# A new written order for the first two chunks of an attention and gated feed-forward kernel

## The chip, the cores and the metric

The kernel runs on one core of one Trainium2 chip. The metric is the device time of one execution in microseconds. The engines are PE (TensorE), DVE (VectorE), ACT (ScalarE), POOL (GpSimd) and SP (SyncE), which issues most transfers; 16 DMA engines carry them. Each engine takes its instructions strictly in the order in which they were emitted.

## The reference

Two parts follow each other. The first is attention over 4 batches of 8 heads, 768 positions of 64 numbers: each position looks at its neighbours closer than 16 and at 24 block summaries (the largest key and the mean value of each block of 32). The second is a feed-forward layer whose hidden row is gated by a three-tap convolution.

```python
k_sum = k.reshape(B, H, nb, block, D).max(axis=3)
v_sum = v.reshape(B, H, nb, block, D).mean(axis=3)
scores_l = where(|i - j| < 16, scale * q @ k.T, -1e9)
scores_s = scale * q @ k_sum.T + log(block)
a = softmax(concat(scores_l, scores_s))
x = a @ concat(v, v_sum)                  # heads joined: (4, 768, 512)
h = maximum(x @ w_in, 0)                  # (4, 768, 1024)
conv = sum over k of conv_w[k] * h shifted by k - 1
out = (h * sigmoid(conv)) @ w_out         # (4, 768, 512)
```

## The kernel before, in words

The work is cut into 8 chunks: batch `c // 2`, first or second half of its positions. Attention goes by pairs of heads, four pairs to a chunk, so pair `n` belongs to chunk `n // 4`; 32 pairs in all. The contraction with `w_in` goes by eighths `u` of the hidden row, and each step `f c.u.cc` is three matmuls of 384 or 386 columns, one for each of the four quarters `cc` of the 512 inputs. The second contraction, with `w_out`, is three matmuls of 512 columns for each 128 positions and each eighth. Weights arrive as 64-bit floats and are taken apart on the chip into two 32-bit parts.

Chunks 0 and 1, together with the attention of pairs 8 to 13 and part of the second contraction of batch 0, are written out as one long string, `ORDER`, in which each word is one step. A function `run` (L542) turns a word into a call, and as the call stands under `manual_schedule` (L553) each engine gets its instructions in just this order. The words:

- `R`, `Q`, `T`, `K`, `V`, `M`, `O` are transfers issued by SP: the transposed keys of a pair (392 KB), its queries (192), its transposed values (384), its key windows (360), its value windows (288), the block means (72), and an eighth of `w_out` (512). `ks` (L268) takes the block maxima of the keys, `vs` (L283) the block sums of the values, both on DVE; `win`, `kb`, `vb` copy into the windows, `pv` and `vm` turn and scale the sums.
- `qk` is the 24 score matmuls of a pair; `mx` (L328, DVE) and `ex` (L343, ACT) are the softmax of a third of a head; `sm` and `rc` invert its sum, `nr` multiplies by it on POOL (`p`) or DVE (`v`); `tr` transposes a head's result on PE and `cp` copies it back on ACT (`a`) or DVE (`v`); `av` multiplies by the values; `xh`, `xl` take the result apart for the contraction.
- `f` as above; `re` rectifies, `ta` multiplies the middle tap (ACT or DVE), two `cv` (L458, DVE) add the outer ones, `th`, `mu`, `gh`, `gl` gate the row and take it apart. `g st.fc` is one step of the second contraction, `ob` stores.
- `zi`, `loi`, `sti`, `hii`, `wli` (and the same with `o`) take one eighth of the weights apart on ACT (L143), DVE (L154, L160), ACT (L175) and POOL (L180). `wN` is N matmuls on zeros, whose result is not used.

Ahead of `ORDER` stand 25 loads in a string of their own, `LOADS` (L559 to L563): keys, queries, values and value windows of pairs 0 to 3, all eight parts of `w_in` and the convolution's weights, and 10 matmuls on zeros.

Chunks 2 to 7 come from loops. `unit(c, u)` (L645) emits one eighth of a chunk. Through `slot(j)` (L571) it emits attention work for later pairs: an even slot the keys and values of pair `n + 2` (`R`, `K`, `T`) and the scores and softmax of pair `n`, an odd one the next queries, and for the first half of a batch `vs`, `pv`, `v_mean` and `k_max` of the pair to come. Here only PE keeps the written order. For SP, DVE, ACT and POOL a planner places the instructions by its own times, and it may put them between the steps of `ORDER` on the same engine, as their buffers allow. Buffers that matter: `kT` and `stage` have two each (`stage` is shared by the `T` loads from pair 8 on, the `O` loads and the key windows of pair 3), `kw` three, `va` and `q` four. A transfer that waits for its buffer holds up all behind it on SP.

Of the kernel before, what the change touches and what calls it, by code (L numbers as in the profile page):

```python
# [52 lines left out]
ex2.1.1 mx2.1.2 cp3a sti1 w1 qk3 O1 ex2.1.2 vs3 R8 hii1 av1 Q7 sm2 wli1 mx3.0.0 O5 rc2 pv3
ex3.0.0 mx3.0.1 R9 mx3.0.2 vm3 xh1 V5 loi2 w1 f0.1.0 ex3.0.2 xl1 nr2.0p M5 ex3.0.1 mx3.1.0
f0.1.1 zi2 vb3 mx3.1.1 mx3.1.2 tr4 zi3 f0.0.1 sti2 ex3.1.2 ex3.1.0 cp4v nr2.1p hii2 loi3 w3 tr5
ex3.1.1 wli2 zi5 sm3 cp5a sti3 w4 av2 zi6 rc3 hii3 loi6 f0.2.0 nr3.0v V6 xh2 wli3 tr6 M6 f0.2.1
cp6a nr3.1v zi7 xl2 kb4 w2 tr7 qk4 sti6 cp7a hii6 loi7 f0.0.2 K7 mx4.0.0 kb5 f0.2.2 ex4.0.0 Q8
sti7 av3 mx4.0.1 wli6 hii7 f0.1.2 ex4.0.1 V7 xh3 loi4 M7 zi4 mx4.0.2 kb6 xl3 wli7 ex4.0.2
# [12 lines left out]
gl0.4 ex7.1.2 f0.7.3 re0.6 mu0.5 tr13 O2 sm7 ta0.6a pv8 loo0 qk8 rc7 vm8 T10 sto0 cp13a f1.0.0
M8 re0.7 nr7.1p cv0.6.0 Q12 hio0 av6 mx8.0.0 K11 cv0.6.2 nr7.0p ta0.7a f1.0.1 mx8.0.1 ex8.0.0
V10 cv0.7.0 wlo0 xh6 tr14 mx8.0.2 zo2 cv0.7.2 ex8.0.2 cp14v g0.0 ex8.0.1 xl6 th0.7 tr15 loo2
g0.1 th0.6 mx8.1.0 O3 sto2 gh0.5 f1.0.2 ex8.1.0 cp15v gl0.5 hio2 mu0.6 av7 mx8.1.1 wlo2 gh0.6
mu0.7 f1.1.0 ex8.1.1 mx8.1.2 V11 vs10 xh7 qk9 gl0.6 ex8.1.2 gh0.7 xl7 f1.2.0 T9 zo3 loo3 K12
f1.0.3 mx9.0.0 gl0.7 sm8 Q13 pv10 ex9.0.0 f1.2.1 O6 re1.0 g0.2 sto3 vm10 ta1.0a M10 rc8 kb11
f1.2.2 mx9.0.1 hio3 nr8.1p cv1.0.0 f1.1.1 ex9.0.1 mx9.0.2 cv1.0.2 nr8.0p f1.2.3 ex9.0.2 mx9.1.0
f1.1.2 th1.0 vs9 wlo3 ex9.1.0 tr16 re1.2 f1.1.3 mx9.1.1 O7 mu1.0 cp16a pv9 kb12 g0.3 ta1.2a
mx9.1.2 re1.1 loo6 f1.3.0 gh1.0 cv1.2.0 tr17 ex9.1.1 gl1.0 ta1.1v g0.4 vm9 zo6 cp17v M9 qk10
cv1.1.0 ex9.1.2 T11 sm9 g0.5 sto6 zo7 Q14 cv1.1.2 f1.3.1 K13 hio6 rc9 av8 th1.1 loo7 mx10.0.0  # L80
wlo6 mu1.1 ex10.0.0 f1.3.2 mx10.0.1 xh8 V12 cv1.2.2 f1.4.0 ex10.0.1 M12 nr9.1p vs11 th1.2 g0.6
gh1.1 nr9.0p f1.4.1 mu1.2 xl8 gl1.1 f1.3.3 gh1.2 mx10.0.2 f1.5.0 ex10.0.2 sto7 tr18 re1.3 f1.5.1
mx10.1.0 gl1.2 ta1.3a cp18v f1.4.2 ex10.1.0 cv1.3.0 pv11 hio7 kb13 f1.5.2 mx10.1.1 cv1.3.2 vm11
wlo7 tr19 ex10.1.1 M11 f1.5.3 mx10.1.2 th1.3 cp19v qk11 ex10.1.2 mu1.3 re1.5 av9 sm10 gh1.3 rc10
K14 mx11.0.0 nr10.0p ta1.5a mx11.0.1 g0.7 mx11.0.2 ex11.0.1 M13 cv1.5.0 nr10.1p xh9 f1.6.0 V13
mx11.1.0 ex11.0.2 cv1.5.2 gl1.3 tr20 ex11.1.0 xl9 f1.6.1 ob0 cp20v f1.4.3 th1.5 mx11.1.1 tr21
ex11.0.0 mx11.1.2 g1.0 ex11.1.2 cp21v re1.4 f1.6.2 ex11.1.1 av10 ta1.4a sm11 cv1.4.0 f1.6.3 xh10
rc11 cv1.4.2 g1.1 nr11.0p re1.6 xl10 th1.4 qk12 nr11.1p ta1.6v mu1.4 g1.2 K15 cv1.6.0 gh1.4 tr22
# [658 lines left out]
```

## Time and profile before

| what | value |
|---|---|
| three runs | 397.14 us median, 397.09 to 398.24 |
| profiled execution | 396.87 us, span 395.1 us |
| PE busy | 376.2 us, 95% of the span |
| DVE, ACT, POOL busy | 252.4, 252.1 and 149.9 us |
| mean granted TensorE clock | 0.991 |
| bytes moved | 56.35 MB |

The span runs from the first to the last instruction; the profiled execution's own time is 1.8 us longer. A busy share is an average over stages with different limits: the written part takes about the first 118 us, the loops the rest. PE's busy time counts the matmuls on zeros too.

### The profile page before, as it was taken

Reading aid. Unit: us, or ns where it says so; the run is one execution under the profiler, and the core shown is the slowest. Engines: PE = TensorE matmul, PEld = TensorE weight load, DVE = VectorE, ACT = ScalarE, POOL = GpSimd, SP = SyncE. Lnnn points to the kernel's source line nnn. Section 1 sums busy time; section 2 is a strip of 40 time slices with the busy share of each in tenths; the row PEclk is TensorE's granted clock in tenths of the full one; section 3 lists DMA queues with packets and bytes.
Section 4 is the critical chain, followed back from the end, with each engine's and each line's share of the span. In section 5 each row is a group of like instructions: output and inputs, shape, how many; then the busy total and the mean of one; then the engine's idle time right before and its main releaser. Section 6 shows DMA issues by size and latency. Waiting matters only on the chain.

```text
span 395.1 us, 8807 instructions
## 1 busy us (share of the span) xinstructions
PE 376.2 (95%) x3148; PEld 315.2 (80%) x3154; DVE 252.4 (64%) x769; ACT 252.1 (64%) x792; POOL 149.9 (38%) x184
## 2 busy tenths in 40 slices
...
GB/s 279 347 379 335 255 309 207 268 241 246 265 209 146 117 95 139 190 144 164 111 107 74 127 69 97 118 105 123 104 37 28 29 0 28 27 28 27 27 55 53
DMA packets 27435, 56.35 MB, mean 143 GB/s; under 512 B 3136, under 2 KB 11520, under 8 KB 27392
## 3 DMA queue, kind: packets, MB, share of 16 engines
...
q8 instruction: 25, 0.41, 0.4%
...
HBM read 47.43 MB, written 6.29 MB: 136 GB/s over the span
## 4 chain that ended last, share of the span: by engine, by line
PE 70%; DVE 10%; DMA 8%; ACT 7%; POOL 2%; issue 2%; SPq 0%; ACTq 0%; POOLq 0%
PE f L508 30%; PE f L424 25%; PE xp L382 5%; PE pt L368 4%; PE pq L314 4%; DMA wo<-w_out 4%; DVE t L458 3%; ACT a L343 2%; DMA vt<-vT 2%; DMA kw<-k_win 1%; DVE ks L268 1%; POOL a L360 1%; PE pw L125 1%; DVE a L328 1%; ACT t L469 1%
## 5 line engine op out<-in xcount | busy, mean ns | idle before, releaser
L489 POOL TENSOR_TENSOR glo<-t,ghi 128x383 fp32r<-128x383 f32 (+1 forms) x64 | 65.8, 1029 | 122.4 <-ACT ghi L486 115.0
L424 PE MATMUL f<-xh,win_hi 128*128 128x384 f32 (+1 forms) x256 | 93.1, 364 | 2.8 <-DVE t L476 2.7
L458 DVE SCALAR_TENSOR_TENSOR t<-f,cw,t 128x382 f32<-128x382 f32 (+3 forms) x128 | 78.7, 615 | 14.5 <-ACT t L447 11.9
L424 PE MATMUL f<-xh,win_lo 128*128 128x384 f32 (+1 forms) x256 | 87.1, 340 | 0.3 <-POOL win_lo L180 0.3
L424 PE MATMUL f<-xl,win_hi 128*128 128x384 f32 (+1 forms) x256 | 87.1, 340 | 0.1
L343 ACT ACTIVATE a<-a,nm 128x120 f32<-128x120 f32 x192 | 73.8, 386 | 14.5 <-DVE nm L328 13.6
L508 PE MATMUL f<-wout_hi,ghi 128*128 128x512 f32 x192 | 76.3, 398 | 0.3 <-ACT ob L518 0.3
L508 PE MATMUL f<-wout_lo,ghi 128*128 128x512 f32 x192 | 75.3, 392 | 0.3 <-POOL wout_lo L180 0.3
L508 PE MATMUL f<-wout_hi,glo 128*128 128x512 f32 x192 | 74.9, 391 | 0.0
L469 ACT ACTIVATE t<-t 128x383 f32<-128x383 f32 (+1 forms) x64 | 33.4, 524 | 45.5 <-DVE t L458 44.4
L360 POOL TENSOR_TENSOR a<-a,sm 128x360 f32<-128x360 f32 x61 | 49.1, 826 | 31.5 <-ACT f L438 16.5
L424 PEld LDWEIGHTS f<-xh,win_hi 128*128 128x128 f32 x256 | 48.7, 190 | 8.2 <-DVE t L476 3.9
L476 DVE SCALAR_TENSOR_TENSOR t<-t,f 128x383 f32<-128x383 f32 (+1 forms) x64 | 35.4, 553 | 28.0 <-ACT t L469 27.7
L424 PEld LDWEIGHTS f<-xl,win_hi 128*128 128x128 f32 x256 | 48.8, 191 | 1.8 <-DVE xl L412 0.5
L424 PEld LDWEIGHTS f<-xh,win_lo 128*128 128x128 f32 x256 | 48.5, 190 | 0.8 <-POOL win_lo L180 0.8
L328 DVE CUSTOM_DVE_ANT_0 a<-pq,mask 128x120 f32<-128x120 f32 x192 | 44.6, 274 | 2.2 <-PE pq L314 2.2
L508 PEld LDWEIGHTS f<-wout_hi,glo 128*128 128x128 f32 x192 | 36.0, 188 | 7.9
L508 PEld LDWEIGHTS f<-wout_hi,ghi 128*128 128x128 f32 x192 | 36.1, 188 | 6.8 <-ACT ob L518 0.9
L508 PEld LDWEIGHTS f<-wout_lo,ghi 128*128 128x128 f32 x192 | 36.2, 188 | 5.7 <-POOL wout_lo L180 0.6
L486 ACT CAST ghi<-t 128x383 fp32r<-128x383 f32 (+1 forms) x64 | 32.5, 509 | 12.1 <-DVE t L476 11.8
L368 PE MATMUL pt<-ident,a 128*120 128x128 f32 x192 | 32.8, 279 | 6.7 <-ACT aT L373 2.8
L438 ACT ACTIVATE f<-f 128x384 f32<-128x384 f32 (+1 forms) x64 | 30.2, 473 | 14.0 <-PE f L424 13.5
...
## 6 DMA issues: line engine op xcount, KB each, us to landing
...
kT<-kT SPq DMA_DIRECT2D x12, 392.0 KB
vt<-vT SPq DMA_DIRECT2D x12, 384.0 KB
...
```

The costliest lines, as they stand in the source:

```text
L328: nc.vector.tensor_tensor_reduce(aa[n, h][:, i, :], pq[n][h][:, i * NK : (i + 1) * NK], mask[:, {(0, 0): 0, (1, 2): 2}.get((hf, i), 1), :] ...
L343: nc.scalar.activation(a, a, AF.Exp, bias=nm[n][:, h, i : i + 1], scale=-1.0, accum_out=sm[n][:, h, i : i + 1],)
L360: engine[e].tensor_tensor(a, a, sm[n][:, h, :].unsqueeze(2).to_broadcast([P, 3, NK]), ALU.mult)
L368: nc.tensor.transpose(pt[j][:NK, i * P : (i + 1) * P], a[:, i, :], ident)
L424: nc.tensor.matmul(f1ps[c, u][:, :n], w[:, u, cc, :], x[:, cc, :n], start=(cc == 0 and m == 0), stop=(cc == NCC - 1 and m == 2),)
L438: nc.scalar.activation(h, h, AF.Relu)
L458: nc.vector.scalar_tensor_tensor(t[:, i0:i1], f1ps[c, u][:, hf + k - 1 + i0 : hf + k - 1 + i1], cw[:, u, k : k + 1], t[:, i0:i1], ALU.mult ...
L469: nc.scalar.activation(t, t, AF.Tanh, scale=0.5)
L476: nc.vector.scalar_tensor_tensor(t, t, 1.0, h, ALU.add, ALU.mult)
L486: nc.scalar.copy(gate_rows("hi", c, u), conv[c, u])
L489: nc.gpsimd.tensor_tensor(gate_rows("lo", c, u), conv.pop((c, u)), gate_rows("hi", c, u).bitcast(F32), ALU.subtract,)
L508: nc.tensor.matmul(f2ps[b, st], g[:, fc, ss], w[:, fc, :], start=(fc == 0 and m == 0), stop=(fc == NFC - 1 and m == 2),)
```

## The change

The loads of `LOADS` move into `ORDER` as words of their own (`C` for the convolution's weights, `I` for the parts of `w_in`), and `ORDER` is written anew: the same steps in another order. The matmuls on zeros go from 10 + 56 to 12 + 35. Of 25 `cp`, 13 ran on DVE and 12 on ACT; now 10 and 15. Of 16 `ta`, 5 ran on DVE; now 4. All other steps are the same in number and on the same engines, though not always for the same pair.

The step functions that issue transfers, and `mu`, now return their instruction, and `run` keeps for each engine the last one returned: on SP the last load of `ORDER` (K15), on DVE mu1.7. In chunk 2 (`FIRST`), what `slot(j)` emits on these two engines is ordered behind them; `issue_after(x)` gives each instruction of the block that runs on the engine of `x` an edge to `x`, without a semaphore.

```diff
-LOADS = "k0 q0 k1 q1 v0 k2 q2 a0 v1 k3 q3 a1 w0 v2 c a2 w1 v3 a3 w2 w3 w4 w5 w6 w7"
-WARM = 10
+WARM = 12
...
 ORDER = """
-ks0 win0 kb0 qk0 ks1 win1 Q4 mx0.0.0 kb1 K4 ex0.0.0 mx0.0.1 mx0.0.2 ex0.0.1 vs0 ex0.0.2 win2
-mx0.1.0 w9 pv0 ks2 ex0.1.0 vm0 mx0.1.1 kb2 ex0.1.1 mx0.1.2 w5 qk1 vb0 ex0.1.2 sm0 rc0 vs1 nr0.1p
...
-ex12.1.1 xh11 qk13 ex12.1.2 xl11 ex12.1.0 f1.7.2 sm12 mx13.0.0 rc12 g1.6 ex13.0.0 mx13.0.1
-nr12.0p mx13.0.2 ex13.0.1 mx13.1.0 f1.7.3 ex13.0.2 nr12.1p mx13.1.1 mx13.1.2 ex13.1.0 g1.7
-ex13.1.2 tr24 ex13.1.1 ob1 cp24v sm13 re1.7 rc13 nr13.0p ta1.7a nr13.1p cv1.7.0 cv1.7.2 th1.7
-mu1.7 gh1.7 gl1.7
+R0 Q0 R1 I0 I1 R2 Q1 ks0 R3 win0 Q2 kb0 qk0 T0 ks1 win1 C kb1 zi0 loi0 T1 mx0.0.0 ex0.0.0
+mx0.0.1 mx0.0.2 sti0 zi1 I6 mx0.1.0 hii0 mx0.1.1 loi1 ex0.0.1 V0 win2 mx0.1.2 ex0.1.0 ks2 w12
+qk1 Q3 ex0.1.2 ex0.1.1 sti1 ex0.0.2 I2 mx1.0.0 kb2 sm0 hii1 mx1.0.1 win3 I4 mx1.0.2 rc0 ex1.0.0
+mx1.1.0 nr0.0p mx1.1.1 ex1.1.0 mx1.1.2 V1 ex1.0.2 vs0 nr0.1p w8 qk2 K4 ex1.0.1 ex1.1.1 wli1 ks3
+tr0 ex1.1.2 pv0 Q4 cp0a mx2.0.0 w1 tr1 mx2.0.1 ex2.0.0 kb3 mx2.0.2 wli0 vm0 vs1 T2 zcw zi6 cp1a
+mx2.1.0 w3 pv1 sm1 vb0 K5 mx2.1.1 ex2.0.1 locw mx2.1.2 ex2.1.0 rc1 w1 qk3 Q5 nr1.0v vm1 ex2.1.2
...
+rc2 sti2 xh0 ex3.0.0 nr2.0v O0 cp3a mx3.0.2 vb1 mx3.1.0 hii6 w4 tr4 mx3.1.1 V3 ex3.0.1 loi4 kb4
+mx3.1.2 cp4a T9 sti4 w2 qk4 hii2 xl0 nr2.1p ex3.1.0 I7 ex3.0.2 vs2 av1 wli6 ex3.1.2 ex3.1.1 I3
...
+gl1.5 xl10 f1.7.3 sm12 cp23a mx13.1.1 th1.6 g1.7 rc12 mx13.1.2 nr12.1p ex13.1.0 mu1.6 av11
+ex13.0.2 nr12.0p re1.7 gh1.6 ta1.7v tr24 ex13.1.2 gl1.6 cv1.7.0 ex13.1.1 ob1 cv1.7.2 th1.7 sm13
+xh11 rc13 mu1.7 nr13.1p xl11 gh1.7 nr13.0p cp24v gl1.7
 """
...
+    def C():
+        words["cw"] = sp.tile([P, 2 * NFC * 3], U32, tag="cww", name="cw_words", bufs=1)
+        return nc.sync.dma_start(words["cw"], cwT.bitcast(U32))
+
-    def load_in(fc):
+    def I(fc):
         t = raw_a[:, fc, :] if fc < 6 else raw_b[:, fc - 6, :]
         words[f"i{fc}"] = t
-        nc.sync.dma_start(t, w_in[fc].bitcast(U32))
+        return nc.sync.dma_start(t, w_in[fc].bitcast(U32))
...
-        steps[name](*map(int, digits.split(".") if digits else []), *letter)
+        x = steps[name](*map(int, digits.split(".") if digits else []), *letter)
+        if x is not None:
+            last[x.ins.engine] = x.ins
...
-        slot(j)
+        with contextlib.ExitStack() as behind:
+            if c == FIRST:
+
+                for x in last.values():
+                    behind.enter_context(tc.issue_after(x))
+            slot(j)
```

## Rows read from the trace of the kernel before

**Rows 1.** The page's first part: busy time, share of the span and instructions of each engine.
```profile
PE 376.2 (95%) x3148; PEld 315.2 (80%) x3154; DVE 252.4 (64%) x769; ACT 252.1 (64%) x792; POOL 149.9 (38%) x184
```

**Rows 2.** Who waited for whom, PE alone, from 120 us to the end: what was waited for, us in total, times, the longest.
```profile
PE pt L368 <- ACT aT L373: 2.2, 2, 1.9
```

**Rows 3.** The timeline of PE: start, us, the instruction. The last matmul of f0.0.3, the last of f1.7.3, the first of f2.0.3.
```profile
40.07 0.34 PE L424 MATMUL f<-xh,win_lo 128*128 128x384 f32 x1
...
116.46 0.34 PE L424 MATMUL f<-xh,win_lo 128*128 128x386 f32 x1
...
120.50 0.34 PE L424 MATMUL f<-xh,win_hi 128*128 128x384 f32 x1
```

**Rows 4.** The chain of waits in the first 125 us, pieces of PE: start, us, what (24 matmuls are one `qk` or one `av`, 3 of L368 one `tr`, 12 of L424 four `f`, 9 of L508 three steps of the second contraction).
```profile
107.56 0.78 PE pq L314 x24
...
119.09 2.10 PE f L424 x12
121.19 2.07 PE f L508 x9
123.26 0.33 PE pt L368 x3
123.59 0.85 PE xp L382 x24
```

**Rows 5.** Busy time by stretches, up to f0.0.3 and from there to f1.7.3: the stretch, its length, busy us (instructions) of PE, PEld, DVE, ACT and POOL, granted clock, DMA share, GB/s.
```profile
4.76:40.41 35.65, 31.56 (x324) 19.60 (x329) 32.37 (x103) 25.91 (x92) 20.82 (x25) 1.00 1.04 358
40.41:116.64 76.23, 69.58 (x675) 55.33 (x677) 68.53 (x215) 63.42 (x206) 45.64 (x52) 0.96 0.84 247
```

**Rows 6.** Who waited for whom, DVE alone, in the first 122 us (columns as in rows 2).
```profile
DVE a L328 <- PE pq L314: 2.2, 3, 1.6
...
DVE wl_o L154 <- DMA wo<-w_out: 1.7, 1, 1.7
DVE vs L283 <- DMA vt<-vT: 1.3, 2, 0.7
```

**Rows 7.** The chain of waits in the first 125 us, other pieces: start, us, what. L343 is `ex`, L373 `cp`, L469 `th`, L458 `cv`, L476 `mu`; the transfers are T8 and O3.
```profile
60.69 0.38 ACT a L343 x2
61.06 0.37 ACT aT L373
...
61.82 0.41 ACT t L469
...
63.53 4.23 DMA vt<-vT
...
72.44 0.53 DVE t L458
72.96 0.47 DVE aT L373
...
74.29 5.59 DMA wo<-w_out
...
93.44 0.47 DVE t L476
```

**Rows 8.** Groups of DVE's instructions from 4.7 to 121.9 us: line, operation, tiles, shapes, count, busy us, mean ns, idle us before them.
```profile
L160 DVE SCALAR_TENSOR_TENSOR wu_i<-wu_i,wl_i 128x512 uint32<-128x512 uint32 x8 | 7.6, 955 | 0.4 <-ACT wu_i L143 0.3
L268 DVE TENSOR_REDUCE ks<-kT 128x24 f32<-128x768 f32 x8 | 7.6, 945 | 0.5 <-POOL kw L277 0.5
...
L160 DVE SCALAR_TENSOR_TENSOR wu_o<-wu_o,wl_o 128x512 uint32<-128x512 uint32 x8 | 6.5, 815 | 0.0
L283 DVE TENSOR_REDUCE vs<-vt 128x24 f32<-128x768 f32 x6 | 5.7, 948 | 1.3 <-DMA vt<-vT 1.3
L154 DVE TENSOR_SCALAR wl_i<-raw_a 128x512 uint32<-128x512 uint32 x6 | 4.8, 797 | 0.0
...
L154 DVE TENSOR_SCALAR wl_o<-wo 128x512 uint32<-128x512 uint32 x8 | 3.3, 416 | 1.7 <-DMA wo<-w_out 1.7
```

**Rows 9.** The timeline of DVE around one `ks`: start, us, the instruction.
```profile
40.28 0.94 DVE L268 TENSOR_REDUCE ks<-kT 128x24 f32<-128x768 f32 x1
41.15 0.60 DVE L449 TENSOR_SCALAR t<-f,cw 128x383 f32<-128x383 f32 x1
```

**Rows 10.** Busy time by stretches, early in the written part and in chunk 2 (columns as in rows 5).
```profile
10.00:40.00 30.00, 26.57 (x288) 17.44 (x291) 27.51 (x90) 23.87 (x85) 18.71 (x21) 1.00 1.04 354
120.00:160.00 40.00, 40.00 (x372) 35.38 (x371) 23.05 (x81) 29.99 (x98) 14.14 (x18) 1.00 0.41 126
```

**Rows 11.** Transfers issued in the first 117 us: destination and source, queue, operation, count, KB each.
```profile
kT<-kT SPq DMA_DIRECT2D x10, 392.0 KB
...
vt<-vT SPq DMA_DIRECT2D x8, 384.0 KB
```

**Rows 12.** The timeline of PE at the first zeros and at 13 zeros later on, and the busy time of the stretches behind the latter (columns as in rows 5).
```profile
1.19 4.45 PE L125 MATMUL pw<-idle 128*128 128x512 bf16 x10 [1.19 <-DVE idle L120]
6.29 1.48 PE L314 MATMUL pq<-kw,q 64*64 64x120 f32 x24 [0.66 <-POOL kw L277]
...
41.12 2.98 PE L125 MATMUL pw<-idle 128*128 128x512 bf16 x13
```
```profile
44.00:48.15 4.15, 1.14 (x8) 0.68 (x8) 4.15 (x16) 3.66 (x14) 2.50 (x2) 0.96 1.05 241
48.15:54.60 6.45, 6.45 (x57) 5.16 (x58) 4.22 (x13) 3.81 (x11) 2.61 (x4) 0.50 1.05 332
```

More of the change, by code (lines that the diff above doesn't have):

```diff
@@ L1 @@
+import contextlib
 import numpy as np
@@ L53 @@
[L53 to L58, printed above, removed]
@@ L71 @@
[L71 to L76, printed above, removed]
@@ L77 @@
[L77 to L88, printed above, removed]
@@ new lines @@
+cp13v gh0.4 O4 g0.1 cv0.6.0 xh5 K10 gl0.4 tr14 re0.7 mx8.1.0 xl5 f1.0.0 ex8.1.0 mx8.1.1 nr7.1p
+gh0.5 av6 cv0.6.2 ex8.0.1 mx8.1.2 kb9 th0.6 ks10 f1.0.1 gl0.5 cp14a qk9 xh6 mu0.6 ta0.7a sto2
+f1.1.0 zo6 xl6 tr15 hio2 f1.1.1 loo6 cp15a mx9.0.0 f1.0.2 wlo2 T11 cv0.7.0 ex8.0.2 Q10 av7
+ex8.1.2 mx9.0.1 cv0.7.2 R11 hio3 f1.1.2 sto6 th0.7 g0.2 xh7 mx9.0.2 wlo3 mu0.7 ex8.0.0 xl7
+f1.2.0 zo4 mx9.1.0 f1.0.3 ex8.1.1 loo4 mx9.1.1 gh0.7 T10 f1.2.1 sto4 sm8 K11 re1.0 f1.1.3 rc8
+gl0.7 vs11 ta1.0a f1.2.2 re1.1 g0.3 cv1.0.0 nr8.0p O5 hio4 mx9.1.2 M8 f1.2.3 gh0.6 cv1.0.2 kb10
@@ new lines @@
+V8 wlo4 ta1.1a pv11 ks11 tr16 ex9.0.2 qk10 th1.0 cv1.1.0 nr8.1p ex9.0.0 g0.4 mu1.0 ex9.1.1 gl0.6
+cv1.1.2 cp16a f1.3.0 vm11 vs10 ex9.1.2 tr17 kb11 f1.3.1 th1.1 ex9.1.0 mx10.0.0 pv10 O7 mu1.1
+f1.3.2 vm10 Q11 zo5 loo5 f1.4.0 V9 mx10.0.1 gh1.0 sto5 f1.3.3 M9 ex9.0.1 cp17v gl1.0 f1.4.1 K12
+re1.2 mx10.0.2 V10 sm9 av8 ta1.2a rc9 mx10.1.0 Q12 nr9.0p ex10.0.2 mx10.1.1 cv1.2.0 Q14 f1.4.2
+nr9.1p zo7 K13 cv1.2.2 tr18 f1.4.3 Q13 mx10.1.2 th1.2 loo7 qk11 hio5 mu1.2 xh8 cp18v wlo5 V11
+f1.5.0 ex10.1.0 mx11.0.0 M10 tr19 xl8 ex10.0.1 f1.5.1 ex10.1.1 sto7 g0.5 hio6 K14 mx11.0.1 hio7
@@ new lines @@
+cp19v wlo6 f1.5.2 mx11.0.2 re1.3 av9 V12 mx11.1.0 ta1.3a mx11.1.1 wlo7 ex10.0.0 g0.6 cv1.3.0 V13
+ex10.1.2 cv1.3.2 f1.5.3 M13 ex11.0.0 kb12 sm10 mx11.1.2 g0.7 gh1.2 rc10 M11 nr10.0p qk12 M12 ob0
+gl1.2 th1.3 tr20 ex11.0.2 g1.0 mu1.3 K15 nr10.1p ex11.1.2 mx12.0.0 f1.6.0 cp20v ex11.1.1 kb13
+gh1.3 g1.1 mx12.0.1 mx12.0.2 ex11.0.1 gl1.3 tr21 re1.4 f1.6.1 re1.5 ta1.4v g1.2 ex11.1.0 cv1.4.0
+xh9 f1.6.2 sm11 mx12.1.0 cp21a mx12.1.1 g1.3 ex12.0.0 rc11 mx12.1.2 nr11.0p cv1.4.2 ta1.5a qk13
+ex12.1.1 th1.4 f1.6.3 ex12.0.2 mu1.4 g1.4 gh1.1 cv1.5.0 ex12.1.0 gl1.1 f1.7.0 xl9 re1.6 tr22
@@ L95 @@
+cv1.5.2 gh1.4 f1.7.1 nr11.1p mx13.0.0 th1.5 cp22v av10 ex13.0.0 gl1.4 mx13.0.1 mu1.5 ex12.0.1
+f1.7.2 ta1.6a mx13.0.2 g1.5 ex12.1.2 cv1.6.0 xh10 tr23 cv1.6.2 gh1.5 g1.6 ex13.0.1 mx13.1.0
+gl1.5 xl10 f1.7.3 sm12 cp23a mx13.1.1 th1.6 g1.7 rc12 mx13.1.2 nr12.1p ex13.1.0 mu1.6 av11
+ex13.0.2 nr12.0p re1.7 gh1.6 ta1.7v tr24 ex13.1.2 gl1.6 cv1.7.0 ex13.1.1 ob1 cv1.7.2 th1.7 sm13
+xh11 rc13 mu1.7 nr13.1p xl11 gh1.7 nr13.0p cp24v gl1.7
 """
@@ L225, in K @@
         c, p, b, hf = at(n)
-        nc.sync.dma_start(keys(n), k_win[c, p])
+        return nc.sync.dma_start(keys(n), k_win[c, p])
     def R(n):
```

59 lines of the change are left out of this document (26 added, 33 removed).

## The prediction

> **What bounds the kernel now.** I read the page's first two parts, then the busy time by stretches, then one engine at a time in the written part, then the chain of waits. The page alone misleads: PE is busy for 95% of the span [rows 1], and only after some 120 us is that all real work. There the chain is PE's own matmuls back to back, PE lost 2.2 us to one pair of waits [rows 2], and none of these matmuls is touched. Whatever the change is worth arises before chunk 2's first contraction begins at 119 us [rows 4].
>
> Before that PE is not short of time. The written list holds 64 `f` steps, 16 `g`, 14 `qk`, 25 `tr`, 12 `av` and a few short `pv`, which I leave out. At full clock one takes 0.525 (2.10 for four), 0.69 (2.07 for three), 0.78, 0.33 and 0.85 us [rows 4]: 33.6 + 11.0 + 10.9 + 8.3 + 10.2 = 74 us of 118. The rest is zeros, waits and half clock. The engine that is full is DVE. I cut the list at two marks: 40.41 and 116.64 us, where f0.0.3 and f1.7.3 are through (their last matmuls start at 40.07 and 116.46 [rows 3]). From the first key maximum at 4.76 us to the second mark DVE is busy 32.4 + 68.5 = 100.9 of 111.9 us (90%), ACT 25.9 + 63.4 = 89.3, POOL 20.8 + 45.6 = 66.5 [rows 5]. Transfers are the second limit: the DMA engines are full up to the first mark [rows 5], DVE waits 1.7 and 1.3 us for `wo` and `vt` [rows 6], and landings of 4.2 and 5.6 us stand on the chain [rows 7].
>
> **DVE: what leaves it.** On `kT` and `vt` tiles the list asks for four `ks` and four `vs` (pairs 8 to 11), yet DVE did eight and six in this part [rows 8]: six sums of later pairs, which the planner had put between the written steps. The change orders them behind mu1.7. One occupies DVE for 0.87 us (the next starts at 41.15 after a start at 40.28) [rows 9]: 5.2 us go. The rest I counted in the two lists up to f1.7.3: three fewer `cp` on DVE (12 to 9) at 0.47, two fewer `ta` (5 to 3) at about 0.53, as a `cv`, and one `mu` and one `xl` fewer at 0.47 each [rows 7]: 1.4 + 1.1 + 0.9 = 3.4, with one `rc` 3.5 us, partly given to ACT and partly put behind the mark. Together 8.7 us. ACT's own list up to the mark grows by only 0.4 us, since some of its steps move behind it.
>
> I hold DVE's idle time as it was, 111.9 - 100.9 = 11.0 us: the list differs, but no row gives a reason for a better or worse fit except those put in the rivals. Then f1.7.3 ends at 116.6 - 8.7 = 107.9 us. ACT would be busy 89.7 of 103.2 us, 87% where it was 80%.
>
> **The seam to chunk 2.** Chunk 2's f2.0.3 began 3.9 us after f1.7.3 ended (120.50 against 116.64) [rows 3]. In the new list xh11 and xl11 stand at the very end, behind mu1.7, and f2.0.3 needs them. From f1.7.3 ACT has one copy, one tanh, two exponentials and then re1.7 (taken as long as a copy): 0.37 + 0.41 + 0.76 + 0.37 = 1.9 us. Then follow ta1.7 0.53, two `cv` 1.06, tanh 0.41, `mu` 0.47 and xl11 0.47 [rows 7], and an estimated 0.7 us for handing on: 5.6 us. PE's own work up to there is 0.69 + 0.85 + 2 x 0.33 + 3 x 0.525 = 3.8, so the chain counts: 1.7 us are lost. Net gain 8.7 - 1.7 = 7.0 us.
>
> **What I cost at nothing.** *The moved sums* then run in chunk 2, where DVE is busy 23.0 of 40 us [rows 10]; 5.2 more make 71%. pv16 comes four units of some 5.3 us into the chunk, so the cover is over 15 us; if it were gone, each late sum would cost its 0.87 us. *The moved loads*: SP issued ten `kT` and eight `vt` loads by 117 us where the list has four and four [rows 11]. Ten of 392 or 384 KB, 3.9 MB, now queue on SP behind K15, and with them chunk 2's other loads. At the 358 GB/s of a full queue [rows 5] they take 11 us of chunk 2's 42, where the DMA engines stand at 0.41 [rows 10]. K15 itself waits only for the `kw` buffer that qk12 frees, some 10 us ahead of the seam. *The new places of loads*: I measured the way from a load's place to its first use in DVE work at 88% occupancy. O2, O3, T8 and T9 had 3.8, 4.4, 5.0 and 4.4 us, hardly what such a load took to land [rows 7]; now 11.5, 9.6, 16.2 and 10.4. Only O7 stays tight (4.3, now 3.9). SP issues in order: T9 waits there for the buffer of pair 3's keys (qk3), T8 for loo0, with I7, I3, K6 and Q6, or I5, K7 and Q7 behind them; their uses lie 9 us or more on. *The zeros*: 66 become 47, 12 of them ahead of qk0. Ten took 4.45 us from 1.19 [rows 12], so twelve end near 6.5; qk0 began at 6.29: 0.2 us, left out.
>
> *DVE beside POOL.* A low-word step takes 416 ns on `wo` but 797 on `raw_a`, a join 815 or 955 [rows 8]. All sixteen low steps at 416 and all joins at 815 would give 3.4 us, all at the long ends cost 4.9. POOL's work is the same, so I take zero, nearest to the mix as it is. [...]
>
> **Forecast.** The profiled execution took 396.87 us, span 395.1 and 1.8 around it; the runs' median, 397.14, is 0.3 above. 396.87 - 7.0 = 389.9, with the median's offset 390. Chunks 2 to 7 add at most the 2.2 us of [rows 2] either way: own range 387 to 393.
>
> **Rivals.**
> *The transfers' waits go too.* With the leads above, DVE's 1.7 + 1.3 us for transfers end, and its 2.2 us for `pq` [rows 6], whose longest fell into a stretch at half clock [rows 12]. 390 - 5.2 = 385. For it: the longer leads. Against: a denser order turns one wait into another.
>
> *TensorE's clock falls early.* [...] From 10 to 40 us it had stayed at 1.00 with PE busy 26.6 of 30 us [rows 10]. In the new list, between pv1 and f0.0.3, PE has 11 zeros (0.23 us each, from 13 in 2.98 [rows 12]) and steps worth 11.4 us: 13.9 us, in a stretch for which DVE needs 20.3 / 0.88 = 23.1 us. At half clock throughout PE needs 27.8: 4.7 us more, 395. For it: only 60% is filled. Against: the gaps are spread, each a microsecond or two. [...]
>
> *PE's order of waiting decides: slower.* Between the two marks PE must do 57 `f`, 15 `g`, 8 `qk`, 16 `tr` and 7 `av`: 58.4 us (57.4 before). It did them in 76.2 us [rows 3], a share of 0.75. My forecast wants them in 107.9 - 41.5 = 66.4 us, 0.88, where 41.5 is f0.0.3 with DVE's list up to it 1.0 us longer. PE takes its steps strictly as written, each `tr` waits for POOL or DVE and each `f` for a PSUM bank; if such waits hold its share at 0.75, f1.7.3 ends at 41.5 + 77.5 = 119.0, 2.4 us later, and with the seam's 1.7 the time is 397 + 4.1 = 401. It decides from a share of 58.4 / 73.4 = 0.80 downwards. Against it: before, DVE and the half clock set that share.
>
> **Chances.** Forecast 0.45, transfers' waits gone too 0.22, clock 0.16, PE's order 0.17. About 1.2 us (0.3%) is what a measurement can tell from no change. The forecast, the better case and most of the clock case are faster: 0.80; within: 0.06; slower: 0.14. The range 383.5 to 397 takes in 385 and 395, with a part of POOL's ends on either side, and leaves out most of the slow case.
>
> **What would show it.** Right: up to f1.7.3 DVE does four `ks` on `kT` and four `vs` on `vt`, the fifth `kT` load follows K15; f1.7.3 ends near 108; DVE idles about 11 us up to there; PE's share between the marks is near 0.88; f2.0.3 waits for xl11. Wrong: a granted clock of 0.5 before 40 us with DVE waiting for PE (clock); a share near 0.75 (order); DVE idle under 7 us (better case). New PE waits for `pv` or `kw` in chunk 2 would show that what moved behind the list was not covered.

## The result, and the profile after

The changed kernel takes 388.38 us (388.10 to 388.70, 4 runs) beside 397.69 us (397.09 to 398.50, 4 runs) before: a ratio of 0.9765, interval 0.9741 to 0.9788. Two later sets on other chips gave 0.9744 (0.9703 to 0.9785) and 0.9731 (0.9685 to 0.9777). The forecast was 390, the direction and the order of size were right; two of its terms were not, and they nearly cancel.

The profiled execution took 388.25 us, its span is 386.5. The page's first part answers to [rows 1]. Lines of the code are now higher, by one up to the weight splits (the low step L155, the join L161) and by five from the transfers on (`f` is L429, `tr` L373, `cp` L378). A low step is `lo`, which takes the low part out of a 64-bit word; a join is `st`, which puts the two parts together.

```profile
PE 367.7 (95%) x3131; PEld 314.4 (81%) x3135; DVE 245.5 (64%) x765; ACT 250.4 (65%) x796; POOL 147.8 (38%) x184
```

PE stands at 95% again, and again that says nothing. What tells is where the three marks of [rows 3] have gone. From the timeline of PE after (start, us, the instruction, and in brackets what it waited for): the last matmul of f0.0.3, the last of f1.7.3, `tr24`, `tr25`, the first of f2.0.0 and the first of f2.0.3.

```profile
37.65 0.52 PE L429 MATMUL f<-xh,win_lo 128*128 128x384 f32 x1
...
102.83 0.34 PE L429 MATMUL f<-xh,win_lo 128*128 128x386 f32 x1
...
104.90 0.54 PE L373 MATMUL pt<-ident,a 128*120 128x128 f32 x3 [0.19 <-POOL a L365]
108.64 0.89 PE L373 MATMUL pt<-ident,a 128*120 128x128 f32 x3 [3.19 <-DVE aT L378]
109.18 0.67 PE L429 MATMUL f<-xh,win_hi 128*128 128x384 f32 x1
...
112.21 0.52 PE L429 MATMUL f<-xh,win_hi 128*128 128x384 f32 x1
```

f1.7.3 is through at 103.0 where it was 116.64: 13.6 us earlier, against a forecast of 8.7. But f2.0.3 starts 9.2 us behind it, where it was 3.9 and 5.6 was forecast: 5.3 us are given back instead of 1.7. What is left, 120.50 - 112.21 = 8.3 us, is nearly the 8.6 us by which the span is shorter; from f2.0.3 to the end it takes 274.3 us, before 274.6.

The busy time by stretches (as in [rows 5]): to f0.0.3, from there to f1.7.3, the seam, the start of chunk 2, and a part of chunk 2.

```profile
4.91:37.97 33.06, 26.21 (x324) 17.59 (x327) 30.57 (x116) 26.77 (x104) 18.85 (x24) 0.96 1.04 364
37.97:103.00 65.03, 63.06 (x629) 53.43 (x628) 56.45 (x187) 59.88 (x194) 43.35 (x51) 0.99 0.81 251
103.00:108.64 5.64, 2.26 (x32) 1.47 (x31) 4.25 (x14) 4.36 (x16) 3.74 (x5) 0.86 0.81 212
108.64:113.97 5.33, 5.33 (x18) 5.19 (x18) 3.91 (x6) 0.95 (x2) 1.54 (x3) 0.51 0.95 317
...
111.70:151.70 40.00, 40.00 (x367) 35.38 (x366) 24.82 (x82) 28.22 (x91) 12.45 (x16) 0.97 0.54 170
```

In the first two rows DVE (third pair) is busy 30.57 + 56.45 = 87.0 of 98.1 us. Its idle time is 11.1 us, just what was held (9.5 and 9.0 us in the profiles of the two later sets); its work is 87.0 instead of 100.9 - 8.7 = 92.2. So 5.2 us more of DVE's work went than the list explains. The groups of DVE in this part (as in [rows 8]) show where:

```profile
L161 DVE SCALAR_TENSOR_TENSOR wu_o<-wu_o,wl_o 128x512 uint32<-128x512 uint32 x8 | 5.6, 699 | 0.2
L161 DVE SCALAR_TENSOR_TENSOR wu_i<-wu_i,wl_i 128x512 uint32<-128x512 uint32 x8 | 5.5, 682 | 0.0
L155 DVE TENSOR_SCALAR wl_o<-wo 128x512 uint32<-128x512 uint32 x8 | 4.5, 558 | 2.3 <-DMA wo<-w_out 2.3
...
L273 DVE TENSOR_REDUCE ks<-kT 128x24 f32<-128x768 f32 x4 | 3.8, 949 | 0.0
L288 DVE TENSOR_REDUCE vs<-vt 128x24 f32<-128x768 f32 x4 | 3.7, 937 | 0.0
L155 DVE TENSOR_SCALAR wl_i<-raw_a 128x512 uint32<-128x512 uint32 x6 | 2.5, 423 | 0.3 <-DMA raw_a<-w_in 0.3
...
L365 DVE TENSOR_TENSOR a<-a,sm 128x360 f32<-128x360 f32 x3 | 1.8, 589 | 0.0
...
L155 DVE TENSOR_SCALAR wl_i<-raw_b 128x512 uint32<-128x512 uint32 x2 | 1.5, 739 | 0.0
L161 DVE SCALAR_TENSOR_TENSOR cw<-cw,wl_cw 128x24 uint32<-128x24 uint32 x1 | 0.2, 170 | 0.0
```

The three of these groups that [rows 8] lacks were, before:

```profile
L360 DVE TENSOR_TENSOR a<-a,sm 128x360 f32<-128x360 f32 x3 | 2.6, 895 | 0.0
...
L160 DVE SCALAR_TENSOR_TENSOR cw<-cw,wl_cw 128x24 uint32<-128x24 uint32 x1 | 1.1, 1080 | 0.0
L154 DVE TENSOR_SCALAR wl_i<-raw_b 128x512 uint32<-128x512 uint32 x2 | 0.9, 445 | 0.0
```

The sums are four and four, as forecast. The other seven groups have the same instructions as before, and took 7.6 + 6.5 + 3.3 + 4.8 + 2.6 + 1.1 + 0.9 = 26.8 us; now 21.6. That is the missing 5.2 us: the steps that met POOL at work before meet it less now. Two timelines of the kernel before show three such meetings, first DVE's, then POOL's:

```profile
29.63 1.59 DVE L160 SCALAR_TENSOR_TENSOR wu_i<-wu_i,wl_i 128x512 uint32<-128x512 uint32 x1
...
35.38 0.69 DVE L160 SCALAR_TENSOR_TENSOR wu_i<-wu_i,wl_i 128x512 uint32<-128x512 uint32 x1
...
53.88 1.55 DVE L160 SCALAR_TENSOR_TENSOR wu_i<-wu_i,wl_i 128x512 uint32<-128x512 uint32 x1
...
55.56 0.94 DVE L268 TENSOR_REDUCE ks<-kT 128x24 f32<-128x768 f32 x1
```
```profile
29.38 1.30 POOL L180 TENSOR_TENSOR win_lo<-wu_i,win_hi 128x512 fp32r<-128x512 f32 x1
...
35.49 1.74 POOL L180 TENSOR_TENSOR win_lo<-wu_i,win_hi 128x512 fp32r<-128x512 f32 x1 [0.52 <-ACT win_hi L175]
...
53.88 2.42 POOL L489 TENSOR_TENSOR glo<-t,ghi 128x383 fp32r<-128x383 f32 x2
```

The join that starts together with a `gl` on POOL takes 1.55 us instead of its 0.69; the block maximum beside the end of the same pair takes its usual 0.94. The other two joins show what decides. At 29.63 us POOL's instruction was there first, and the join ends 0.54 us after POOL's. At 35.38 the join was there first: it takes 0.69, and POOL's instruction 1.74 us instead of 1.30. So it is in the whole part: 11 of the 16 joins took 0.67 to 0.69 us before, the other five 1.04 to 1.60, and all five had POOL's instruction running or starting with them. After, the longest join takes 0.78 us.

DVE's own waits up to 108 us (as in [rows 6]) are others now, though its idle time up to f1.7.3 is the same:

```profile
DVE ks L273 <- DMA k_xh<-kT: 4.3, 2, 3.9
DVE t L481 <- ACT t L474: 3.9, 3, 2.4
DVE wl_o L155 <- DMA wo<-w_out: 2.3, 3, 1.0
DVE t L454 <- ACT f L443: 1.6, 3, 0.8
```

Its waits for `vt` (1.3) and for `pq` (2.2) are gone; `mu` now waits 3.9 us for ACT's tanh, and `wo` costs 2.3 instead of 1.7.

### The profile page after: what moved, and what is told of

Same layout as the page of the kernel before. It is cut to its first block, busy times and chain, and to the rows that moved or that the text cites. A ratio compares the mean times of both kernels' runs of the same rounds, so it can differ in the third digit from the quotient of the medians.

```text
span 386.5 us, 8769 instructions
## 1 busy us (share of the span) xinstructions
PE 367.7 (95%) x3131; PEld 314.4 (81%) x3135; DVE 245.5 (64%) x765; ACT 250.4 (65%) x796; POOL 147.8 (38%) x184
## 4 chain that ended last, share of the span: by engine, by line
PE 74%; DMA 13%; DVE 5%; ACT 5%; issue 1%; POOL 0%; SPq 0%; ACTq 0%; DVEq 0%; POOLq 0%
PE f L513 31%; PE f L429 29%; DMA wo<-w_out 6%; PE xp L387 5%; PE pt L373 5%; PE pq L319 4%; DMA kw<-k_win 2%; DMA va<-v_win 2%; DVE t L463 2%; DMA raw_b<-vT 2%; ACT a L348 2%; ACT t L474 1%; DMA mask<-mask 1%; DVE t L481 1%; DVE ks L273 1%
## 5 line engine op out<-in xcount | busy, mean ns | idle before, releaser
L494 POOL TENSOR_TENSOR glo<-t,ghi 128x383 fp32r<-128x383 f32 (+1 forms) x64 | 65.0, 1016 | 121.2 <-ACT ghi L491 112.4
L429 PE MATMUL f<-xh,win_hi 128*128 128x384 f32 (+1 forms) x256 | 93.7, 366 | 0.6 <-DVE t L481 0.3
L429 PE MATMUL f<-xl,win_hi 128*128 128x384 f32 (+1 forms) x256 | 87.9, 343 | 0.0
L429 PE MATMUL f<-xh,win_lo 128*128 128x384 f32 (+1 forms) x256 | 87.6, 342 | 0.0
L429 PEld LDWEIGHTS f<-xh,win_hi 128*128 128x128 f32 x256 | 49.3, 192 | 5.6 <-DVE t L481 1.7
L429 PEld LDWEIGHTS f<-xl,win_hi 128*128 128x128 f32 x256 | 49.4, 193 | 1.3 <-DVE xl L417 0.2
L429 PEld LDWEIGHTS f<-xh,win_lo 128*128 128x128 f32 x256 | 49.2, 192 | 0.0
L373 PE MATMUL pt<-ident,a 128*120 128x128 f32 x192 | 33.2, 282 | 6.8 <-DVE aT L378 3.2
```

The costliest lines, as they stand in the source:

```text
L373: nc.tensor.transpose(pt[j][:NK, i * P : (i + 1) * P], a[:, i, :], ident)
L429: nc.tensor.matmul(f1ps[c, u][:, :n], w[:, u, cc, :], x[:, cc, :n], start=(cc == 0 and m == 0), stop=(cc == NCC - 1 and m == 2),)
L494: nc.gpsimd.tensor_tensor(gate_rows("lo", c, u), conv.pop((c, u)), gate_rows("hi", c, u).bitcast(F32), ALU.subtract,)
```

## The experiments

**The two halves apart.** The change orders the steps anew and puts chunk 2's loads and sums behind the list. One kernel has only the new order:

```diff
-            if c == FIRST:
+            if False:
```

> The changed kernel without the edges behind the last load and mu1.7; the new order stays. Theory (DVE's work sets the written part, the six moved sums are worth 0.87 us each there): the planner puts sums of pairs 16 to 19 between the written steps again, f1.7.3 ends 3 to 5 us later than 103.0 us, and the time is 391 to 393.5 us. Rival (the sums only fill waits of DVE, the new order alone does it): 388.4 within 0.8 us.

Measured: 392.48 us, 0.9881 (0.9847 to 0.9915). The time and f1.7.3 (through at 106.3 us) are as expected, the way is not: only two sums of later pairs came into the written part, not six. But each of them did worse than occupy DVE. From the timeline of DVE in this kernel:

```profile
86.34 0.95 DVE L273 TENSOR_REDUCE ks<-kT 128x24 f32<-128x768 f32 x1 [1.73 <-POOL kw L282]
...
91.71 0.95 DVE L273 TENSOR_REDUCE ks<-kT 128x24 f32<-128x768 f32 x1 [2.94 <-POOL kw L282]
```

A `ks` of pairs 16 and 17 writes into a buffer that the `kb` of an earlier pair on POOL must have read. The two stood in DVE's queue 4.7 us too early (1.73 and 2.94), and DVE took nothing past them in that time. f1.7.3 is through 3.3 us later than in the kernel with the edges. DVE's work up to there is 88.2 us instead of 87.0 (the two sums are 1.9, other steps are shorter), its idle time 13.6 instead of 11.1. So the edges are worth more than the sums that they move.

The other kernel has the old order with the 25 loads in front of it, and the edges:

```diff
-LOADS = "k0 q0 k1 q1 v0 k2 q2 a0 v1 k3 q3 a1 w0 v2 c a2 w1 v3 a3 w2 w3 w4 w5 w6 w7"
...
+R0 Q0 R1 Q1 T0 R2 Q2 V0 T1 R3 Q3 V1 I0 T2 C V2 I1 T3 V3 I2 I3 I4 I5 I6 I7 ks0 win0 kb0 qk0 ks1 win1
...
+                for x in last.values():
+                    behind.enter_context(tc.issue_after(x))
```

> The old order with its loads in front and its 10 + 56 zeros, and only the edges added. Theory (DVE's work): six sums leave DVE ahead of f1.7.3, which ends some 5 us earlier than 116.6, time 391 to 393.5 us, a ratio of 0.984 to 0.990. Rival (the sums only fill waits): 396.5 to 398, ratio 1.00. Both kernels' gains together then say whether order and edges add up to the change's 9 us.

Measured: 392.89 us, 0.9903 (0.9876 to 0.9931). The two halves, 1.2% and 1.0%, add up to nearly the whole, 2.4 to 2.7%. Where f1.7.3 ends they are less alike: 10.3 us earlier with the order alone, 1.5 with the edges alone, where some 5 were expected, 13.6 with both; the order alone then loses at the seam, where f2.0.3 comes 9.4 us behind f1.7.3. The busy time by stretches in this kernel up to f1.7.3 (its profiled execution, 395.01 us, was the longest of ten):

```profile
4.76:115.10 110.34, 99.46 (x995) 74.40 (x999) 92.83 (x312) 88.88 (x297) 66.17 (x77) 0.97 0.79 258
```

DVE's work fell by 100.9 - 92.8 = 8.1 us, but f1.7.3 came only 1.5 us earlier: DVE's idle time rose from 11.0 to 17.5. In the old order less work on DVE is mostly turned into waiting; the new order is what lets the end follow DVE. How large that part is rests on this one profile: the median of the ten is 2.1 us shorter. It also tells where the 5.2 us come from. The seven groups take 23.6 us here and 21.2 in the kernel with only the new order, 26.8 before and 21.6 after: each half brings fewer meetings with POOL, the order more. Joins of `wu_i` here still take 854 ns and the `cw` join 1078; with only the new order they take 687 and 171. What in the new order lets the end follow DVE (the places of the steps and loads, the copies that went to ACT, the fewer zeros) was not taken apart.

**DVE beside POOL, measured by itself.** At the end of the changed kernel, twelve low steps and twelve joins run on DVE, the first six of each alone, the second six beside ten multiplications of a 128x512 tile by itself on POOL. Their results are not used; the kernel was executed once.

```diff
+        lows(6)
+        joins(6)
+        nc.vector.tensor_copy(a, low.bitcast(F32))
+        for _ in range(10):
+            nc.gpsimd.tensor_tensor(o, a, a, ALU.mult)
+        lows(6)
+        joins(6)
```

> The changed kernel with work added at its end, beside PE's last contraction, whose results are not used: on DVE six low-word steps and six joins of 512 words as in the weight splits, with POOL idle, and then the same again while POOL does ten tensor_tensor of 512 numbers on other tiles. Theory (what made DVE's steps short in the new order is that they meet POOL less): alone a low step takes about 420 ns and a join about 690, beside POOL a low step 700 to 1300 and a join 900 to 1600. Rival (they were long in the old order for another reason, transfers or the strided reads): the same durations in both halves within 10%.

What the trace tells of the lines L696 (low steps), L700 (joins) and L711 (POOL), first up to 366.6 us, then from 367 us on; the three numbers are the shortest, the median and the longest in ns:

```profile
L696 DVE TENSOR_SCALAR probe_low<-probe_w x6: 421/428/1126, 358.9 to 361.9; 128x512 uint32<-128x512 uint32 x6
...
L700 DVE SCALAR_TENSOR_TENSOR probe_u<-probe_u,probe_low x6: 691/692/694, 362.4 to 366.0; 128x512 uint32<-128x512 uint32 x6
...
L696 DVE TENSOR_SCALAR probe_low<-probe_w x6: 428/1145/1147, 367.1 to 372.2; 128x512 uint32<-128x512 uint32 x6
...
L700 DVE SCALAR_TENSOR_TENSOR probe_u<-probe_u,probe_low x6: 691/1412/1414, 373.4 to 380.7; 128x512 uint32<-128x512 uint32 x6
...
L711 POOL TENSOR_TENSOR probe_o<-probe_a x10: 1100/1191/1371, 367.1 to 378.7; 128x512 f32<-128x512 f32 x10
```

Here there are two durations and nothing between: 428 or 1145 for a low step, 692 or 1412 for a join, 0.72 us more in both. POOL's multiplications have two as well, behind the first of 1278: five of 1100 to 1104 beside the low steps, four of 1368 to 1371 beside the joins. Five of the six steps are long in either row beside POOL. The one long step in the first row fell beside the kernel's last `gl` (359.94 to 361.13 us on POOL). The joins are held up beside POOL, with two tiles read, and so are the low steps, with one; the `ks` at 55.56 us in the kernel before is not (0.94 us). A step that is held up ends a fixed time after POOL's instruction: a join 0.54 or 0.55 us, a low step 0.28 or 0.29, in the kernel before and in the changed one. With the same times here, each long step began with an estimated 0.86 us of a multiplication left (1.145 less 0.285, 1.412 less 0.545). In the kernel before there are durations between the two as well, because steps began at different points of POOL's instructions.

**The seam.** `tr25`, the first step of chunk 2's loop, waits 3.19 us for `cp24`: the transposes have one PSUM buffer, and `cp24` stood last in DVE's list, behind mu1.7 and xl11. One kernel moves it forward:

```diff
-ex13.0.2 nr12.0p re1.7 gh1.6 ta1.7v tr24 ex13.1.2 gl1.6 cv1.7.0 ex13.1.1 ob1 cv1.7.2 th1.7 sm13
-xh11 rc13 mu1.7 nr13.1p xl11 gh1.7 nr13.0p cp24v gl1.7
+nr12.1p ex13.1.0 mu1.6 av11 ex13.0.2 nr12.0p re1.7 gh1.6 ta1.7v tr24 ex13.1.2 gl1.6 cv1.7.0 cp24v
+ex13.1.1 ob1 cv1.7.2 th1.7 sm13 xh11 rc13 mu1.7 nr13.1p xl11 gh1.7 nr13.0p gl1.7
```

> The changed kernel with one word moved: cp24v stands behind cv1.7.0 and not at DVE's end. Theory (PE's 3.2 us at the seam are the single buffer that tr25 needs and cp24v frees, and the half clock after it follows from that wait): tr25 starts at about 106.2 instead of 108.6, f2.0.3 waits less than 1 us for xl11, the clock stays at 1.00 or falls for under 2 us: 384 to 385.5 us. Rival (the seam is held by xl11 in any case, as the prediction had it): f2.0.3 waits what tr25 waited before, the clock falls as it did, and the time is 386.5 to 388.4.

Measured: 384.11 us, 0.9689 (0.9639 to 0.9739). From its timeline of PE:

```profile
104.33 0.54 PE L371 MATMUL pt<-ident,a 128*120 128x128 f32 x3 [0.65 <-DVE aT L376]
...
107.09 0.44 PE L427 MATMUL f<-xl,win_hi 128*128 128x384 f32 x1 [0.32 <-DVE xl L415]
```

The wait falls to 0.65 us, the granted clock stays at 1.00 from 100 to 110 us, and now f2.0.3 does wait for xl11, by 0.32 us. A second kernel takes that away too:

```diff
-ex13.0.2 nr12.0p re1.7 gh1.6 ta1.7v tr24 ex13.1.2 gl1.6 cv1.7.0 ex13.1.1 ob1 cv1.7.2 th1.7 sm13
-xh11 rc13 mu1.7 nr13.1p xl11 gh1.7 nr13.0p cp24v gl1.7
+nr12.1p ex13.1.0 mu1.6 av11 ex13.0.2 nr12.0p re1.7 gh1.6 ta1.7v tr24 xh11 ex13.1.2 gl1.6 cv1.7.0
+cp24v ex13.1.1 ob1 cv1.7.2 xl11 th1.7 sm13 rc13 mu1.7 nr13.1p gh1.7 nr13.0p gl1.7
```

> As e3a, with xh11 put behind tr24 on ACT and xl11 behind cv1.7.2 on DVE, both ahead of mu1.7. Theory: nothing at the seam waits for DVE's last steps any more, PE idles about 1 us there, granted clock 1.00: 383.5 to 384.8 us. Rival (xl11 is not late once cp24v is early): the same as e3a within 0.5 us.

Measured: 380.79 us, 0.9614 (0.9570 to 0.9658), 3.3 us below the one before and better than expected (four executions of each, whose intervals just overlap). The 0.32 us at f2.0.3 explain little of that. The rest lies far behind the seam: in the profile with `cp24` alone PE's old wait for ACT near 190 us (1.85 us here, [rows 2] in the kernel before) is followed by a stretch at half clock, which this one does not have. The busy time by stretches, with `cp24` alone:

```profile
186.00:198.00 12.00, 10.15 (x87) 9.34 (x86) 7.34 (x26) 7.06 (x23) 3.78 (x5) 0.86 0.26 80
```

A clock of 0.86 over 12 us is 1.7 us of work not done. With 0.6 us for a `kT` load that the other does not wait for, this is 2.3 of the 2.9 us between the two spans. Two of the four executions with `cp24` alone had a mean clock of 0.999 and 1.000; they took 382.2 and 383.4 us. The kernel with all three steps moved is the fastest here. Run again beside the changed kernel on one chip:

> The changed kernel as it is, a third time, as the base of the two runs beside it on this chip. Theory (a 3.2 us wait of TensorE at the seam, then a stretch at half clock): 0.974 to 0.977 of before, 386 to 388.5 us, and in the profile the wait of 3.2 us ahead of tr25 again.

> The mended seam without zeros (cp24, xh11, xl11 moved forward), now beside after on one chip. Theory: 0.961 to 0.966 of before, 380 to 383.5 us, and 4 to 6 us below after; TensorE's wait of about 1.8 us near 185 to 195 us (pt waiting for ACT's aT) stays at the full clock, as in the first run of it. Rival (the earlier lead of e3b over e8 was the chip's): within 0.2% of e9_seam_zeros.

Measured: 386.18 us, 0.9731 (0.9685 to 0.9777), and 381.64 us, 0.9624 (0.9571 to 0.9678): 4.5 us apart, as expected. Timelines of PE at the seam, first of the kernel as changed, then with the three steps moved:

```profile
106.77 0.54 PE L373 MATMUL pt<-ident,a 128*120 128x128 f32 x3 [3.16 <-DVE aT L378]
...
109.33 0.52 PE L429 MATMUL f<-xh,win_hi 128*128 128x384 f32 x1
```
```profile
103.74 0.54 PE L371 MATMUL pt<-ident,a 128*120 128x128 f32 x3 [0.65 <-DVE aT L376]
...
105.69 0.34 PE L427 MATMUL f<-xh,win_hi 128*128 128x384 f32 x1
```

Of the 4.7 us between the two spans (384.2 and 379.5), 3.6 stand in the last rows of the two, where f2.0.3 begins (0.5 of them were there at f1.7.3); most of the rest is the half clock behind it (0.52 us a matmul instead of 0.34).

**What the clock has in it.** Fourteen matmuls on zeros, results unused, fill the wait at the seam (the trace holds 13 of them):

```diff
-ex13.0.2 nr12.0p re1.7 gh1.6 ta1.7v tr24 ex13.1.2 gl1.6 cv1.7.0 ex13.1.1 ob1 cv1.7.2 th1.7 sm13
+nr12.1p ex13.1.0 mu1.6 av11 ex13.0.2 nr12.0p re1.7 gh1.6 ta1.7v tr24 y14 ex13.1.2 gl1.6 cv1.7.0
...
+    def y(n):
+        t = ps.tile([P, 512], F32, tag="s", name="zeros", bufs=2)
+        for _ in range(n):
+            nc.tensor.matmul(t, idle[:, :P], idle, start=True, stop=True)
```

> The changed kernel unaltered, as the measure for the three beside it on the same chip: ratio 0.974 to 0.979 to the kernel before. In its profile PE waits some 2.1 to 2.4 us ahead of av3 near 32 us and some 3.2 us at the seam near 105 us; the granted clock falls after the second, and after the first only in some executions.

> The changed kernel with 14 zeros behind tr24 in a score buffer (a step y14), so that PE is not idle while tr25 waits for cp24v. The wait itself stays. Theory (half clock behind the wait is a loss of its own, some 2.3 us: the 12 + 9 matmuls after it took 3.84 + 2.38 us where 2.10 + 2.07 is their time): granted clock 1.00 across the seam, 386 us on the chip of the first result, a ratio 0.005 lower than the changed kernel beside it. Rival (what is lost is the wait alone, the half clock falls where PE has slack): no difference beyond 0.002.

Measured on one chip: 386.92 us, 0.9744 (0.9703 to 0.9785), and with the zeros 384.93 us, 0.9701 (0.9664 to 0.9739). From the timeline of PE with the zeros:

```profile
103.52 2.97 PE L413 MATMUL zeros<-idle 128*128 128x512 bf16 x13
106.63 0.54 PE L371 MATMUL pt<-ident,a 128*120 128x128 f32 x3
...
108.58 0.34 PE L432 MATMUL f<-xh,win_hi 128*128 128x384 f32 x1
```

The difference is near the 0.005 expected, though the two intervals overlap. `tr25` comes no earlier behind f1.7.3 than before (5.6 us, as in the first profile of after), but f2.0.3 follows it 1.95 us later, at full clock, instead of 3.57 in the first profile of after (3.52 and 2.56 in the other two). So up to f2.0.3 the half clock costs 0.6 to 1.6 us. In the first profile the 9.2 us of the seam are 1.6 of half clock, 2.5 of wait and the 5.05 us that the kernel with three steps moved needs; moving them saves both losses.

The same was tried at an earlier wait. In the first profile of after, PE stands still for 2.40 us before `av3` at 34.28 us (for the `xp` buffer that `xl` on DVE frees), and from there to 38.50 us the mean granted clock is 0.63. Nine zeros stand there instead:

```diff
-mx5.0.2 vb3 xl2 K7 hio0 mx5.1.0 wli4 ex5.0.2 w1 av3 Q7 mx5.1.1 vs9 ex5.0.1 ex5.1.0 f0.0.2
...
+w9 av3 Q7 mx5.1.1 vs9 ex5.0.1 ex5.1.0 f0.0.2 mx5.1.2 xh3 M4 loi7 f0.1.2 zi7 xl3 sm4 sti7 ex5.1.2
```

> The changed kernel with 9 more zeros ahead of av3, where PE waited 2.4 us for xl2. Theory (that wait drops the clock in some executions and then costs 1 to 2 us, since PE and DVE are both full behind it): clock 1.00 from 30 to 45 us, ratio 0.001 to 0.004 lower than the changed kernel beside it. Rival (PE has slack there): the same within 0.002. If the zeros make PE late: 0.002 higher.

Measured: 389.59 us, 0.9812 (0.9778 to 0.9847), slower than the 386.92 beside it: a miss. But its trace shows the seam once more, with the same wait and no fall of the clock; from its timeline of PE, `tr25` and the first of f2.0.3:

```profile
106.33 0.55 PE L371 MATMUL pt<-ident,a 128*120 128x128 f32 x3 [3.19 <-DVE aT L376]
...
108.28 0.34 PE L427 MATMUL f<-xh,win_hi 128*128 128x384 f32 x1
```

That is 1.95 us again, as with the zeros at the seam. The same nine zeros beside the mended seam:

> The kernel of e3b (cp24v, xh11, xl11 moved) with the 9 zeros of e5 ahead of av3. Theory: both hold side by side, 0.959 to 0.962 of the kernel before, 380 to 381.5 us, granted clock 1.00 throughout. Rival (the zeros do nothing): that of e3b, 0.961 within 0.002.

Measured: 383.83 us, 0.9676 (0.9638 to 0.9714), a miss too. In both traces, as in that of the zeros at the seam, the clock falls behind the wait near 190 us, which it does not in the three profiles of the changed kernel. First the nine zeros alone, then the changed kernel (third set), busy time by stretches:

```profile
186.00:198.00 12.00, 10.01 (x83) 8.85 (x84) 7.63 (x26) 6.55 (x23) 3.68 (x6) 0.86 0.31 102
```
```profile
186.00:198.00 12.00, 10.13 (x93) 8.70 (x92) 8.44 (x26) 6.50 (x23) 4.03 (x6) 1.00 0.31 102
```

I took the zeros for the cause of that and tried the pair once more on one chip:

> The same seam with nine zeros ahead of av3. The zeros' results are unused. Theory (the zeros' 2.3 us shift nothing useful, and the wait near 190 us then ends in 3.4 us at half clock, as it did in all three kernels with added zeros): 0.4 to 0.8% above e9_seam, 383 to 385 us, and the row of granted clock shows a fall behind the wait near 190 us. Rival (the fall near 190 us is chance, not the zeros' doing): the clock stays full there or falls in e9_seam too, and the two times agree within 0.2%.

Measured: 383.67 us, 0.9669 (0.9622 to 0.9716), 0.5% above the same kernel without zeros (381.64), six executions each, which overlap (382.4 to 386.1 and 380.3 to 384.8). The size is the expected one, but the reason falls: in this trace the clock stays at 1.00 near 190 us, and with `cp24` moved alone it fell there with no zeros added. The whole difference of the two spans (380.6 and 379.5) is there at f1.7.3 already, which comes 1.0 us later. In the kernels run beside these, the wait before `av3` was 1.7 to 1.8 us and the clock held behind it: there was no fall for the zeros to prevent. Beside the seam as it is, their loss of 2.7 us in the median lies elsewhere. In that profile, of the fastest of its six executions, f1.7.3 is through at 100.7 us, 1.2 earlier than in the changed kernel beside it, and f2.0.3 begins 2.7 earlier; from there to the end it takes 278.1 us instead of 274.4. Of these 3.7 us, 1.7 are the half clock near 190 us and 1.3 are longer waits of PE for ACT and POOL between 121 and 127 us. Why those come with the zeros, and what decides on the clock near 190 us, stays open.

## Why the prediction was right, and where it was not

*What bounds the written part.* Right: with the end of f1.7.3 at 103.0, DVE is busy 89% of the part, its idle time is 11.1 us where 11.0 was held, and the end moved by what DVE's work shrank. The kernel with the edges alone shows that this was not a property of DVE but of the order: there the idle time grew to 17.5 us and ate most of the gain. In the two later profiles of the changed kernel it was 9.5 and 9.0. Holding it was a guess that came out.

*What leaves DVE.* The six sums went as counted: four `ks` and four `vs` in the part. The list's 8.7 us are in the 13.9 by which DVE's work fell.

*"DVE beside POOL": the term that was mis-sized first.* It was taken as zero, with ends of -3.4 and +4.9 around it, and the rest was held as it was. It measured -5.2: low steps and joins alone, -3.5 (from 7.6 + 6.5 + 4.8 + 0.9 + 3.3 = 23.1 to 5.5 + 5.6 + 2.5 + 1.5 + 4.5 = 19.6), and the `cw` join and three `nr` on DVE, which the bounds left out, -1.7. The ends were none: means of 416 to 955 ns were read as prices, and each is a mix of the time that a step takes alone (some 0.43 us a low step, 0.69 a join) and of longer ones, set by how much of POOL's instruction is left when the step begins. Alone, all 32 steps would take 17.9 us instead of 23.1. The single steps in the timelines of the kernel before, beside POOL's, would have shown it.

*The seam: the step that failed.* "f2.0.3 waits for xl11" named the wrong wait. The chain through xl11 was worked out as 5.6 us, but DVE's list has `cp24` behind xl11, and `tr25`, ahead of chunk 2's first `f`, needs its PSUM buffer. So all of chunk 2 waited, not its fourth quarter, PE stood still for 3.2 us and went on at half clock (0.51 over 5.33 us). The seam cost 5.3 us instead of 1.7; moving one word takes back 2.5 us of the wait (3.19 to 0.65) and the half clock. In that kernel f2.0.3 does wait for xl11, and begins 5.1 us behind f1.7.3 (101.23 to 106.33), where 5.6 was worked out: the sum was sound, for a wait that came second. Of the 5.3 us, 2.5 are the wait for `cp24` and 1.6 the half clock; 1.2 stay with all three steps moved (5.05 against 3.9).

*What was costed at nothing.* Right. From f2.0.3 on the two kernels take 274.3 and 274.6 us. In chunk 2 DVE is busy 24.8 of 40 us where 71% was allowed, the DMA share is 0.54, and the profile has no wait of PE from 112 to 165 us. The fifth `kT` load comes behind K15 (90.26 and 94.21 in the timeline of SP's queue):

```profile
90.26 0.39 SPq L231 DMA_DIRECT2D kw<-k_win  x1
...
94.21 0.43 SPq L239 DMA_DIRECT2D kT<-kT  x1
```

*The rivals.* The transfers' waits did not go as a whole: those for `vt` and `pq` did, but `wo` still costs 2.3 us, and ACT's tanh a new 3.9. TensorE's clock fell early in one of three profiles of after, to a mean of 0.63 over 4.2 us and only after a wait of 2.40 us; where the wait was 1.75 us it held. In these two, f1.7.3 came 1.2 and 1.8 us earlier, on other chips, which is the most that it can be taken to have cost; it was not the 4.7 us of that rival. PE's order of waiting did not decide: PE did the 58.4 us of steps in 65.0, a share of 0.90 where 0.88 was wanted and 0.80 was the point. (By the prices given there the steps come to 57.8 us, a share of 0.89; nothing hangs on it.)

*The sum.* -13.6 + 5.3 = -8.3 against -8.7 + 1.7 = -7.0. The time came within half a percent because -4.9 and +3.6 stood against each other, not because the terms were good.
